# Zero passes on TensorE at the start, a third buffer in the early function, and 65 instead of 96 columns in the q' products

## The chip, the cores and the metric

The kernel runs on one core of one Trainium2 chip. The metric is the device time of one execution in microseconds (us), lower is better. TensorE is written PE in the profile, its weight loads PEld, VectorE DVE, ScalarE ACT, GpSimd POOL and SyncE SP. PE's clock has two levels here, 1.2 and 2.4 GHz.

## The reference

Three stages follow each other, all in float32. First comes a linear attention with random features (q, k, v of shape 2 x 8 x 576 x 64, 128 features):

```
h   = x_s @ omega.T - sum(x_s*x_s)/2          # x_s = q or k, scaled by 64**-0.25
phi = exp(h - max(h, -1)) / sqrt(128)         # gives q' and k'
kv  = k'.T @ v ;  z = sum over tokens of k'
out = (q' @ kv) / (q' @ z + 1e-6)
```

Its output, seen as 1152 tokens of 512 channels, is x of the second stage: `h = x @ w_in` (2048 wide), `g = h - tanh(h)`, `x = g @ w_out`. The third stage is a mixture of four dense experts: for each expert `relu(x @ w1[e]) @ w2[e]`, weighted by each token's normalised probability and summed.

## The kernel before

Products of weights and activations split every float32 operand in a high and a low part and add three products (high by high, high by low, low by high). The features are made by `features`: PE transposes blocks of 128 tokens (`psT`), ACT and DVE split them (`th`, `tl`, the helper `split`, lines 71 and 72), PE multiplies them by the transposed omega `ob` (`psP`), DVE takes the row maximum with its sign turned (`nm`, line 298), and ACT takes the exponential (`kf` or `qf`, line 302). `k_products` multiplies k' by v and by a block of ones (`psV`), so that z stands in the columns behind kv, and DVE copies the first `ZC` columns of each of four blocks to `kvz` (line 319). `q_products` transposes q' (`psQ`, copied by ACT to `qt`), and multiplies it by `kvz` (`psN`, line 348: 128 products of `ZC` = 96 columns, of which 65 are used; line 352: 32 products of half the weights with 65 columns). DVE adds 1e-6, takes the reciprocal and multiplies (lines 354 to 356), PE transposes back (`psX`), and ACT and DVE split the result to `x`, the second stage's input.

The first loads are issued by SP in program order: omega, two blocks of k (`kn`), the rest of k (`kr`, 128 tokens), v, and so on. PE's first work is the transpose of omega (`pso`), then four blocks of `kn`, then `kr` and the other blocks.

While the last q' units run, the second stage begins: `early` makes g = h - tanh(h) for three token ranges (512, 384 and 256 tokens) of the first four hidden blocks, twelve units in all. Its function `minus_tanh` has ten steps. For small h a polynomial is used and for others h - tanh(h): u (ACT: square of h), q (ACT, to y), t (ACT: tanh), m (ACT, a mask in u), a and b (DVE: the polynomial in y), s (DVE: h - tanh, line 453), c (DVE: copy s over y where u is not zero, line 454), h (ACT: high part) and l (POOL: low part, line 456). Before, s writes over h in the PSUM tile `pse`, and t, u and y have two buffers each.

Weights of the second stage arrive in a coded form of 64 bits: ACT and DVE decode them (`Decoded`: `y`, and `m` on lines 122, 126 and 127), ACT makes the high part and POOL the low part (`wal`, `wbl`, line 72).

Up to about 126 us the order of instructions on each engine is set by a scheduler that plans with its own costs. So a change of a size or of a buffer also moves instructions that the diff does not name. From there on PE, DVE and ACT follow an order written out in the program.

Of the kernel before, what the change touches and what calls it, by code (L numbers as in the profile page):

```python
# [8 lines left out]
F32 = mybir.dt.float32  # L9
F32R = mybir.dt.float32r  # L10
I32 = mybir.dt.int32
U32 = mybir.dt.uint32
AF = mybir.ActivationFunctionType
ALU = mybir.AluOpType
# [12 lines left out]
def tile_favor_attention__then__two_moe(  # L27
# [18 lines left out]
    nc = tc.nc  # L46
    B, H, S, D = q.shape
# [3 lines left out]
    E, _, F = w1.shape  # L51
    P = 128
# [21 lines left out]
    def run(todo):  # L74
        for step in todo:
            step()
# [107 lines left out]
    a2 = actx.enter_context(tc.tile_pool(name="a2", bufs=2))  # L184
    a3 = actx.enter_context(tc.tile_pool(name="a3", bufs=3))
    ps_t = actx.enter_context(tc.tile_pool(name="ps_t", bufs=2, space=bass.MemoryType.PSUM))
    ps_n = actx.enter_context(tc.tile_pool(name="ps_n", bufs=2, space=bass.MemoryType.PSUM))
    ps_p = actx.enter_context(tc.tile_pool(name="ps_p", bufs=2, space=bass.MemoryType.PSUM))
    kctx = ExitStack()
    kp = kctx.enter_context(tc.tile_pool(name="kp", bufs=2, side="right"))  # L190
    TD = TB * D
    VC = D + 1
    ZC = D + D // 2
    FULL = slice(0, TB * P)
    REST = slice(TB * P, S)

    def load_full(x, b, p, to):

        nc.sync.dma_start(out=to, in_=x[b, 2 * p:2 * p + 2, FULL, :].rearrange("h (r t) d -> r h (t d)", t=TB))
# [8 lines left out]
    def load_k(p):  # L208
        t = kp.tile([P, B, 2, TD], F32, tag="kn", name="kn")
        for b in range(B):  # L210
            load_full(k, b, p, t[:, b])
        return t
# [19 lines left out]
    def load_v(p):  # L232
        t = vs[p % 2]
        for b in range(B):
            load_full(v, b, p, t[:, b * 2 * TD:(b + 1) * 2 * TD].rearrange("p (h x) -> p h x", h=2))
            r = t[b * D:(b + 1) * D, VR + b * 2 * D:VR + (b + 1) * 2 * D].rearrange("p (h d) -> p h d", h=2)
            nc.sync.dma_start(out=r, in_=v[b, 2 * p:2 * p + 2, REST, :].rearrange("h r d -> r h d"))
# [8 lines left out]
    load_v(0)  # L246
    kn.append(load_k(1))
    load_v(1)

    pso = ps_t.tile([P, 512], F32, tag="t", name="pso")  # L250
    nc.tensor.transpose(pso[:, :P], om.rearrange("p j d -> p (j d)"), ident)
    oms = kp.tile([P, P], F32, name="oms", bufs=1)
    nc.scalar.mul(oms, pso[:, :P], scale)
# [3 lines left out]
    for j in range(2):  # L257
        r, c = slice(j * D, (j + 1) * D), slice(j * P, (j + 1) * P)
        split(ob[0][r, c], ob[1][r, c], oms[r, :])
    qn = ac.tile([P, B, H, TD], F32, name="qn")  # L260
    kvz = [ac.tile([P, B, 2, ZC], F32, name=f"kvz{p}") for p in range(NP)]

# [45 lines left out]
    def k_products(p, kf):  # L308
# [3 lines left out]
        def product(b, h):  # L312
# [5 lines left out]
            if (b, h) == (B - 1, 1):  # L318
                nc.vector.tensor_copy(kvz[p], ps[:, :, :, :ZC])
                if p + 2 < NP:  # L320
# [4 lines left out]
    def q_products(p, gs, qf):  # L325
# [15 lines left out]
        def attended(g):  # L341
            t0, c = gs[g]
            ps = ps_n.tile([P, 2, 2, P], F32, tag="n", name="psN")
            for j in range(c):
                t = t0 + j
                for h in range(2):
                    if t != TB:
                        nc.tensor.matmul(ps[:, j, h, :ZC], qt[g][:, j, h, :], kvz[p][:, t // (TB + 1), h, :], start=True, stop=True)  # L348
                        continue
# [68 lines left out]
    gs, po_of = {}, {}  # L418
# [5 lines left out]
    def new_g(i, j):  # L424
        pool = late["hpb"] if i % 2 or i >= NA else hpa
        gs[i, j] = tuple(pool.tile([P, N], F32R, tag="h" + z, name="h" + z) for z in "hl")

    def hidden(i, j, chunks=range(NC), bank=None, kks=range(KD)):
        if bank is None and chunks[0] == 0 and kks[0] == 0:
            ph[i, j] = late["ps_hb" if j % 2 else "ps_ha"].tile([P, NC, 512], F32, tag="h", name="psh")  # L430
        wh, wl = wa[i, j]
        for kk in kks:
            c = slice(kk * P, (kk + 1) * P)
            xh, xl = state["x"][kk]
            for z, (w, x) in enumerate(((wh, xh), (wh, xl), (wl, xh))):
                for n in chunks:
                    nc.tensor.matmul(  # L437
                        ph[i, j][:, n, :CH] if bank is None else bank, w[:, c],
                        x[:, n * CH:(n + 1) * CH] if bank is None else x[:, n],
                        start=z == 0 and kk == 0, stop=z == 2 and kk == KD - 1,  # L440
                    )

    def minus_tanh(ps, hh, hl, t, u, y, view, eng_lo):

        vec, act = nc.vector, nc.scalar
        return dict(
            u=lambda: act.activation(view(u), ps, AF.Square),
            q=lambda: act.activation(y, u, AF.Square, bias=ca),  # L448
            t=lambda: act.activation(view(t), ps, AF.Tanh),
            m=lambda: act.activation(u, u, AF.Relu, bias=ct),  # L450
            a=lambda: vec.scalar_tensor_tensor(out=y, in0=y, scalar=CB, in1=u, op0=ALU.add, op1=ALU.mult),  # L451
            b=lambda: vec.scalar_tensor_tensor(out=view(y), in0=view(y), scalar=C2, in1=ps, op0=ALU.mult, op1=ALU.mult),  # L452
            s=lambda: vec.tensor_tensor(out=ps, in0=ps, in1=view(t), op=ALU.subtract),  # L453
            c=lambda: vec.copy_predicated(view(y), view(u).bitcast(I32), ps),  # L454
            h=lambda: act.activation(hh, y, AF.Copy),  # L455
            l=lambda: (eng_lo or vec).tensor_tensor(out=hl, in0=y, in1=hh.bitcast(F32), op=ALU.subtract),  # L456
        )

    def activated(i, j, eng_lo=None):
        new_g(i, j)  # L460
        hh, hl = gs[i, j]
        ps = ph[i, j][:, :, :CH]
        if i < NA:
            t, u, y = (late["gp"].tile([P, N], F32, tag=z, name=z, bufs=1 + (z == "y")) for z in "tuy")
            g = minus_tanh(ps, hh, hl, t, u, y, grid, eng_lo)

            for n in range(NC):
                s = slice(n * CH, (n + 1) * CH)
                part = minus_tanh(ps[:, n], hh[:, s], hl[:, s], t, u[:, s], y[:, s], lambda z: z, eng_lo)
                g.update({x + str(n): part[x] for x in "chl"})  # L470
            return g
        return [
            lambda: nc.scalar.activation(grid(hh), ps, AF.Relu),
            lambda: nc.vector.scalar_tensor_tensor(  # L474
                out=grid(hl), in0=ps, scalar=0.0, in1=grid(hh).bitcast(F32), op0=ALU.max, op1=ALU.subtract
            ),
        ]

    def early(e):

        j, n = e % NJ, e // NJ
        if n == 0:
            new_g(0, j)
        s = slice(chunks[n][0][0] * P, (chunks[n][-1][0] + chunks[n][-1][1]) * P)
        w = s.stop - s.start
        pool, tag = (ps_p, "p") if e in (NP + 1, NP + 3, 2 * NP + 1) else (ps_e, "e")
        ps = pool.tile([P, 512], F32, tag=tag, name="pse")[:, :w]
        hidden(0, j, [s], ps)
        t, u, y = (a2.tile([P, 512], F32, tag=z, name=z)[:, :w] for z in "tuy")
        g = minus_tanh(ps, gs[0, j][0][:, s], gs[0, j][1][:, s], t, u, y, lambda z: z, nc.gpsimd)  # L490
        run(g[x] for x in "utqambsch" + "l")

    NU = len(q_units)
    for u in range(1, NU + 3):
        q_emit(u, "R", 0)
        q_emit(u - 1, "A", 0)
        q_emit(u - 2, "Z", 0)
        q_emit(u + 1, "T", 0)
        q_emit(u, "R", 1)
        q_emit(u - 1, "A", 1)  # L500
        q_emit(u - 2, "Z", 1)
        q_emit(u - 3, "X", 0)
        if u >= NP + 3:
            early(u - NP - 3)
        if u in LATER:
            ready(*LATER[u])
        if u == NU + 1:
            ready(load_a, wa, 1, 0)
    for e in range(NU - NP, NU):
        early(e)  # L510
        if e < NU - 2:
            ready(load_a, wa, 1, e % NJ + 1)
# [3 lines left out]
    for b in range(B):  # L516
        for t0, t1, r0, r1, s in token_rows(b):
            nc.sync.dma_start(
                out=pr[r0:r1, t0:t1, :],
# [192 lines left out]
    with tc.manual_schedule(engines={mybir.EngineType.DVE, mybir.EngineType.PE, mybir.EngineType.Activation}):  # L712
        coming = loads(0)
        opened(coming)
        g, left = None, []
        for n, (sh, so) in enumerate(order):
# [29 lines left out]
            g = activated(*steps[sh])  # L746
# [18 lines left out]
    for n in range(NC):  # L765
        s = slice(n * CH, (n + 1) * CH)
# [163 lines left out]
```

## Time and profile before

| | us |
|---|---|
| median of 3 runs | 681.74 |
| lowest and highest | 681.52, 682.08 |
| profiled execution | 681.03 |
| its span | 678.9 |

Of the span PE is busy for 666.2 us (98%), PEld 621.5, DVE 529.8, ACT 317.5, POOL 62.3. PE is called busy from the first to the last of a row of matmuls that follow each other closely, so a busy PE can still run at half its clock; the distance between the starts of two matmuls tells that. The page's line of the granted clock is at 9 tenths or more in all 40 slices; on the first 10 us the text below comes back to it. A row of the timeline gives start, duration, engine, line, what is written and read, and the count where several are merged; the bracket behind it tells how long the engine stood before it, and what released it.

### The profile page before, as it was taken

What the parts mean: (1) busy time and instruction counts of PE and PEld (TensorE: products, weight loads), DVE (VectorE), ACT (ScalarE), POOL (GpSimd) and SP (SyncE); (2) the same over time, 40 slices, a digit from 0 to 9 for tenths busy, and PEclk for the clock granted to TensorE, in tenths of its full rate; (3) what the DMA queues carried; (4) which work ended last, traced back from release to release, by engine and by line L of the source; (5) the groups of instructions that cost most, each with busy time, mean ns of one, the idle gap of its engine ahead of it and who ended that gap; (6) DMA issues with size and microseconds to landing.
All of it is one profiled execution on the core that took longest, in us unless ns stands there. A gap on an engine that the chain in (4) does not pass through costs nothing.

```text
span 678.9 us, 10154 instructions
## 1 busy us (share of the span) xinstructions
PE 666.2 (98%) x4059; PEld 621.5 (92%) x4059; DVE 529.8 (78%) x828; ACT 317.5 (47%) x593; POOL 62.3 (9%) x58
## 2 busy tenths in 40 slices
PE   6999999999999999999999999999999999999997
PEld 5999989999999999998999999998998999999986
DVE  4599889799999988968377777777777777777664
ACT  5699988857767756444122322222232223222120
POOL 1032023413212200100000000000000000000000
PEclk9999999999999999999999999999999999999999
DMA  8953201122322222121001111210202111110004
GB/s 225 281 169 119 67 32 32 32 62 95 94 63 93 78 79 63 31 63 32 1 31 63 32 49 45 63 33 32 63 31 63 32 63 32 36 58 1 1 0 140
DMA packets 42767, 43.73 MB, mean 64 GB/s; under 512 B 5600, under 2 KB 37600, under 8 KB 42720
## 3 DMA queue, kind: packets, MB, share of 16 engines
q1 hardware_dynamic: 42720, 43.08, 20.7%
q8 instruction: 32, 0.52, 0.3%
q14 instruction: 15, 0.12, 0.1%
HBM read 40.72 MB, written 2.36 MB: 63 GB/s over the span
## 4 chain that ended last, share of the span: by engine, by line
PE 79%; DVE 11%; ACT 5%; issue 2%; DMA 2%; SPq 1%; DVEq 0%
PE po L671 29%; PE Y L654 23%; PE po L550 7%; PE psh L437 7%; PE pse L437 4%; PE psP L296 3%; PE psN L348 2%; DVE m L127 1%; DVE m L126 1%; DVE y L451 1%; DVE y L452 1%; DVE y L454 1%; DVE psh L453 1%; ACT y L448 1%; PE psQ L337 1%
## 5 line engine op out<-in xcount | busy, mean ns | idle before, releaser
L677 DVE SCALAR_TENSOR_TENSOR oacc<-po,pr,oacc 128x512 f32<-128x512 f32 (+1 forms) x136 | 101.4, 746 | 34.3 <-PE po L671 33.8
L671 PE MATMUL po<-wbh,hl 128*128 128x512 f32 x290 | 113.0, 389 | 0.4 <-DVE hl L474 0.4
L671 PE MATMUL po<-wbh,hh 128*128 128x512 f32 x290 | 112.9, 389 | 0.1
L671 PE MATMUL po<-wbl,hh 128*128 128x512 f32 x290 | 112.9, 389 | 0.0
L671 PEld LDWEIGHTS po<-wbh,hl 128*128 128x128 f32 x290 | 54.4, 188 | 12.3 <-DVE hl L474 0.8
L671 PEld LDWEIGHTS po<-wbh,hh 128*128 128x128 f32 x290 | 54.7, 188 | 8.2 <-DVE oacc L677 0.3
L842 ACT ACTIVATE hh<-Y 128x576 fp32r<-128x576 f32 x42 | 27.4, 652 | 72.5 <-DVE Y L839 64.0
L671 PEld LDWEIGHTS po<-wbl,hh 128*128 128x128 f32 x290 | 54.4, 188 | 7.5
L550 PE MATMUL po<-hh,wbh 128*128 128x384 f32 x180 | 60.8, 338 | 0.3
L550 PE MATMUL po<-hl,wbh 128*128 128x384 f32 x180 | 60.7, 337 | 0.3 <-DVE hl L456 0.2
L550 PE MATMUL po<-hh,wbl 128*128 128x384 f32 x180 | 60.4, 336 | 0.0
L654 PE MATMUL Y<-y,wah 128*128 128x288 f32 x336 | 57.9, 294 | 0.0
L437 PE MATMUL psh<-x,wah 128*128 128x384 f32 x288 | 57.7, 336 | 0.0
L654 PEld LDWEIGHTS Y<-y,wah 128*128 128x128 f32 x336 | 51.2, 188 | 3.6 <-DVE hl L474 0.3
L437 PEld LDWEIGHTS psh<-x,wah 128*128 128x128 f32 x288 | 50.5, 188 | 0.0
L654 PE MATMUL Y<-Th,wal 128*128 128x288 f32 x224 | 47.9, 295 | 0.0
L654 PE MATMUL Y<-Tl,wah 128*128 128x288 f32 x224 | 47.6, 294 | 0.0
L654 PE MATMUL Y<-Th,wah 128*128 128x288 f32 x224 | 47.6, 293 | 0.0
L842 ACT ACTIVATE hh<-u 128x576 fp32r<-128x576 f32 x14 | 9.6, 687 | 73.5 <-DVE u L839 73.5
L654 PEld LDWEIGHTS Y<-Th,wah 128*128 128x128 f32 x224 | 39.0, 188 | 4.5
L455 ACT ACTIVATE hh<-y 128x1152 fp32r<-128x1152 f32 (+3 forms) x26 | 20.6, 796 | 41.4 <-DVE y L454 41.4
L624 ACT ACTIVATE wah<-y 128x512 fp32r<-128x512 f32 x28 | 17.6, 631 | 41.1 <-DVE y L604 41.1
(138 smaller groups left out, 1472.7 us busy)
## 6 DMA issues: line engine op xcount, KB each, us to landing
raw<-in_moe_w_dram SPq DMA_DIRECT2D x30, 512.0 KB, 3.5
raw<-in_moe_w_in_dram SPq DMA_DIRECT2D x16, 512.0 KB, 3.6
raw<-in_moe_w_out_dram SPq DMA_DIRECT2D x16, 512.0 KB, 3.4
kn<-in_k_dram SPq DMA_DIRECT2D x8, 256.0 KB, 3.9
vs<-in_v_dram SPq DMA_DIRECT2D x8, 256.0 KB, 4.3
qn<-in_q_dram SPq DMA_DIRECT2D x8, 256.0 KB, 4.9
out_dram<-oacc SPq DMA_DIRECT2D x7, 256.0 KB, 2.2
raw<-in_moe_w_dram SPq DMA_DIRECT2D x4, 256.0 KB, 3.2
```

The lines of the kernel that those rows point to most:

```text
L126: nc.vector.scalar_tensor_tensor(out=m, in0=self.y.bitcast(I32), scalar=3, in1=m, op0=ALU.logical_shift_left, op1=ALU.bitwise_or)
L127: nc.vector.scalar_tensor_tensor(out=m, in0=self.up, scalar=SIGN, in1=m, op0=ALU.bitwise_and, op1=ALU.bitwise_or)
L296: nc.tensor.matmul(ps[:, i].rearrange("p a m -> p (a m)"), x[:, c], o, start=j == 0, stop=j == 2)
L348: nc.tensor.matmul(ps[:, j, h, :ZC], qt[g][:, j, h, :], kvz[p][:, t // (TB + 1), h, :], start=True, stop=True)
L437: nc.tensor.matmul(ph[i, j][:, n, :CH] if bank is None else bank, w[:, c], x[:, n * CH:(n + 1) * CH] if bank is None else x[:, n], start=z ...
L455: h=lambda: act.activation(hh, y, AF.Copy),
L550: nc.tensor.matmul(po[:, :CH], w[:, r], g[:, s], start=j == 0 and z == 0, stop=j == NJ - 1 and z == 2,)
L624: nc.scalar.activation(w[0], src, AF.Copy)
L654: nc.tensor.matmul(ps[:, m, :HN // 2], w[:, kk], b[:, m * HN // 2:(m + 1) * HN // 2], start=first and kk == 0 and z == 0, stop=kk == 1 and ...
L671: nc.tensor.matmul(po, g[:, s], w[:, cols], start=j == 0 and z == 0, stop=j == 1 and z == 2)
L677: nc.vector.scalar_tensor_tensor(out=acc, in0=po, scalar=pr[:, t, e:e + 1], in1=acc, op0=ALU.mult, op1=ALU.add)
L842: nc.scalar.activation(halves(gs[NA + q, f][0][:, h * HN:(h + 1) * HN]), x, AF.Relu)
```

## The change

Three edits. (1) A tile of 128 x 256 zeros is filled by DVE, and PE multiplies it by itself 14 times ahead of everything else, into a PSUM tile of the pool `ps_n` that nothing reads. (2) In `early`, s writes its difference over the tanh in tile t instead of over h in PSUM, c reads it there, and y has three buffers instead of two. (3) `ZC` is 65 instead of 96, so line 348's products stream 65 columns, and the copy to `kvz` moves 260 elements a partition instead of 384.

```diff
-    ZC = D + D // 2
+    ZC = VC
...
+    zero = kp.tile([P, 2 * P], F32R, name="zero", bufs=1)
+    nc.vector.memset(zero.bitcast(F32), 0.0)
+    idle = ps_n.tile([P, 512], F32, tag="n", name="idle")
+
+    def busy(n):
+
+        for _ in range(n):
+            nc.tensor.matmul(idle[:, :2 * P], zero[:, :P], zero, start=True, stop=True)
+
 
     pso = ps_t.tile([P, 512], F32, tag="t", name="pso")
+    with tc.high_priority():
+        busy(14)
     nc.tensor.transpose(pso[:, :P], om.rearrange("p j d -> p (j d)"), ident)
...
-    def minus_tanh(ps, hh, hl, t, u, y, view, eng_lo):
+    def minus_tanh(ps, hh, hl, t, u, y, view, eng_lo, free=False):
+
 
         vec, act = nc.vector, nc.scalar
+        d = view(t) if free else ps
...
-            s=lambda: vec.tensor_tensor(out=ps, in0=ps, in1=view(t), op=ALU.subtract),
-            c=lambda: vec.copy_predicated(view(y), view(u).bitcast(I32), ps),
+            s=lambda: vec.tensor_tensor(out=d, in0=ps, in1=view(t), op=ALU.subtract),
+            c=lambda: vec.copy_predicated(view(y), view(u).bitcast(I32), d),
...
-        t, u, y = (a2.tile([P, 512], F32, tag=z, name=z)[:, :w] for z in "tuy")
-        g = minus_tanh(ps, gs[0, j][0][:, s], gs[0, j][1][:, s], t, u, y, lambda z: z, nc.gpsimd)
+        t, u, y = (a2.tile([P, 512], F32, tag=z, name=z, bufs=2 + (z == "y"))[:, :w] for z in "tuy")
+        g = minus_tanh(ps, gs[0, j][0][:, s], gs[0, j][1][:, s], t, u, y, lambda z: z, nc.gpsimd, free=True)
```

PE at the program's start, before and then after (line numbers behind the edit are higher by 11 to 13):

```order
L251 MATMUL pso<-ident,om 128x128
L284 MATMUL psT<-ident,kn 128x128 x4
L284 MATMUL psT<-ident,kr 128x128
L284 MATMUL psT<-ident,kn 128x128 x3
L296 MATMUL psP<-ob_130,th 128x256 x2
```

```order
L256 MATMUL idle<-zero 128x256 x14
L262 MATMUL pso<-ident,om 128x128
L295 MATMUL psT<-ident,kn 128x128 x4
L295 MATMUL psT<-ident,kr 128x128
L295 MATMUL psT<-ident,kn 128x128 x3
L307 MATMUL psP<-ob_147,th 128x256 x2
```

The 14 passes stand ahead of the transpose of omega; the order behind them is the same.

DVE between the third and the fourth copy to `kvz`, before and then after (nm: row maxima; tl: low part of a transposed block; m: decoding of weights):

```order
L319 COPY kvz_141<-psV 128x384
L298 TENSOR_REDUCE nm<-psP 128x4
L127 SCALAR_TENSOR_TENSOR m<-raw,m 128x512
L298 TENSOR_REDUCE nm<-psP 128x4
L72 TENSOR_TENSOR tl<-psT,th 128x512
L126 SCALAR_TENSOR_TENSOR m<-y,m 128x512
L122 TENSOR_SCALAR m<-raw 128x512
L298 TENSOR_REDUCE nm<-psP 128x4
L127 SCALAR_TENSOR_TENSOR m<-raw,m 128x512
L126 SCALAR_TENSOR_TENSOR m<-y,m 128x512
L72 TENSOR_TENSOR tl<-psT,th 128x512
```

```order
L330 COPY kvz_158<-psV 128x260
L309 TENSOR_REDUCE nm<-psP 128x4
L127 SCALAR_TENSOR_TENSOR m<-raw,m 128x512
L309 TENSOR_REDUCE nm<-psP 128x4
L126 SCALAR_TENSOR_TENSOR m<-y,m 128x512
L72 TENSOR_TENSOR tl<-psT,th 128x512
L127 SCALAR_TENSOR_TENSOR m<-raw,m 128x512
L122 TENSOR_SCALAR m<-raw 128x512
L309 TENSOR_REDUCE nm<-psP 128x4
L126 SCALAR_TENSOR_TENSOR m<-y,m 128x512
L122 TENSOR_SCALAR m<-raw 128x512
L72 TENSOR_TENSOR tl<-psT,th 128x512
```

One more decoding step of line 122 stands ahead of the fourth copy, and a tl comes one step later.

DVE in an early unit of 512 tokens, before and then after (steps a, b, s and c are lines 451 to 454, then 464 to 467):

```order
L451 SCALAR_TENSOR_TENSOR y<-y,u 128x512
L355 RECIPROCAL rd<-rd 128x2
L355 RECIPROCAL rd<-rd 128x4
L452 SCALAR_TENSOR_TENSOR y<-y,pse 128x512
L453 TENSOR_TENSOR pse<-pse,t 128x512
L356 TENSOR_TENSOR xs<-psN,rd 128x128
L454 COPY_PREDICATED y<-u,pse 128x512
```

```order
L464 SCALAR_TENSOR_TENSOR y<-y,u 128x512
L365 TENSOR_SCALAR rd<-psN 128x2
L465 SCALAR_TENSOR_TENSOR y<-y,pse 128x512
L466 TENSOR_TENSOR t<-pse,t 128x512
L366 RECIPROCAL rd<-rd 128x2
L365 TENSOR_SCALAR rd<-psN 128x4
L467 COPY_PREDICATED y<-u,t 128x512
```

Step c now reads u and t, both in SBUF; before, one of its two inputs was in PSUM.

## Rows read from the trace of the kernel before

**Rows 1.** Busy time by stretch: length, then each engine's busy us and count

```profile
core 0: us, PE busy (x) PEld busy (x) DVE busy (x) ACT busy (x) POOL busy (x), PEclk, DMA share, GB/s
14.00:31.00 17.00, 16.56 (x140) 16.01 (x138) 9.47 (x17) 11.64 (x41) 0.00 (x0) 1.00 0.91 271
31.00:51.00 20.00, 18.80 (x157) 18.01 (x157) 19.96 (x35) 18.92 (x55) 6.53 (x5) 1.00 0.62 188
51.00:126.00 75.00, 74.98 (x562) 70.19 (x563) 65.73 (x169) 68.11 (x178) 19.72 (x18) 1.00 0.18 57
126.00:679.00 553.00, 547.96 (x3160) 510.12 (x3158) 430.11 (x598) 212.48 (x307) 33.79 (x23) 1.00 0.16 51
```

**Rows 2.** Timeline of the first 9 us, DVE and PE

```profile
0.87 0.55 DVE L256 MEMSET ob<- 128x256 f32 x2 [0.87 <-PEq L914]
...
2.79 0.45 PE L251 MATMUL pso<-ident,om 128*128 128x128 f32 x1 [2.79 <-DMA om<-in_omega_dram]
...
4.52 1.11 PE L284 MATMUL psT<-ident,kn 128*128 128x128 f32 x4 [1.28 <-DMA kn<-in_k_dram]
...
7.62 0.45 PE L284 MATMUL psT<-ident,kr 128*128 128x128 f32 x1 [1.99 <-DMA kr<-in_k_dram]
7.86 0.85 PE L284 MATMUL psT<-ident,kn 128*128 128x128 f32 x3
```

**Rows 3.** Timeline from 8.7 us: how the first features are made

```profile
8.75 0.92 ACT L71 ACTIVATE th<-psT 128x512 fp32r<-128x512 f32 x2 [1.95 <-PE psT L284]
...
9.38 0.89 DVE L72 TENSOR_TENSOR tl<-psT,th 128x512 fp32r<-128x512 f32 x2 [1.87 <-ACT th L71]
...
10.45 1.52 DVE L298 TENSOR_REDUCE nm<-psP 128x4 f32<-128x512 f32 x2 [0.19 <-PE psP L296]
...
10.97 0.28 PE L296 MATMUL psP<-ob,tl 128*128 128x256 f32 x1
...
11.18 2.17 ACT L302 ACTIVATE kf<-psP,nm 128x128 f32<-128x128 f32 x8 [1.51 <-DVE nm L298]
```

**Rows 4.** The same view as rows 1, behind the last matmul

```profile
676.00:681.00 5.00, 0.00 (x0) 0.00 (x0) 0.00 (x0) 0.00 (x0) 0.00 (x0) 0.88 0.11 35
```

**Rows 5.** Timeline from 20 us: SP's issues, and who waits for one

```profile
20.55 0.37 SPq L199 DMA_DIRECT2D vs<-in_v_dram  x1
...
24.66 0.47 SPq L103 DMA_DIRECT2D raw<-in_moe_w_in_dram  x1
...
30.70 0.43 DVE L122 TENSOR_SCALAR m<-raw 128x512 int32<-128x512 int32 x1 [2.31 <-DMA raw<-in_moe_w_in_dram]
```

**Rows 6.** DVE's groups by shape, 0 to 137 us: busy us, mean ns

```profile
L298 DVE TENSOR_REDUCE nm<-psP 128x2 f32<-128x256 f32 x8 | 3.4, 422 | 2.1 <-PE psP L296 2.1
...
L319 DVE COPY kvz<-psV 128x384 f32<-128x384 f32 x4 | 2.2, 548 | 0.2 <-PE psV L314 0.2
```

**Rows 7.** Timeline of PE, one q' unit

```profile
60.34 0.60 PE L337 MATMUL psQ<-ident,qf 128*128 128x128 f32 x4
60.77 1.03 PE L348 MATMUL psN<-kvz,qt 128*128 128x96 f32 x8
```

**Rows 8.** Waits from 68 to 126 us: us in total, times, longest

```profile
ACT y L448 <- POOL hl L456: 1.1, 2, 0.9
```

**Rows 9.** Timeline: DVE steps beside a POOL subtraction, and one without

```profile
74.64 1.27 POOL L72 TENSOR_TENSOR wal<-m,wah 128x512 fp32r<-128x512 f32 x1 [6.67 <-ACT wah L71]
...
75.20 1.26 DVE L126 SCALAR_TENSOR_TENSOR m<-y,m 128x512 int32<-128x512 int32 x1
...
81.16 0.68 DVE L126 SCALAR_TENSOR_TENSOR m<-y,m 128x512 int32<-128x512 int32 x1
...
116.96 1.29 POOL L72 TENSOR_TENSOR wal<-m,wah 128x512 fp32r<-128x512 f32 x1 [0.29 <-ACT wah L71]
117.37 0.60 DVE L454 COPY_PREDICATED y<-u,pse 128x384 f32<-128x384 int32 x1 [0.52 <-ACT u L450]
```

**Rows 10.** The instructions of line 122: ns min/median/max, first and last start

```profile
L122 DVE TENSOR_SCALAR m<-raw x11: 398/428/1516, 30.7 to 80.7; 128x512 int32<-128x512 int32 x11
```

## The prediction

> **What bounds the kernel now.** I read the busy times by stretch first, then the timeline of the start, then the groups by shape and the waits of the stretches that the change touches. The busy times by stretch [rows 1] show that PE has next to no gap once it runs: it stands still for 17.00 - 16.56 = 0.44 us between 14 and 31 us, for 1.20 us between 31 and 51, and for 0.02 us in the 75 us after that. From 126 us on the change touches nothing, and PE is busy for 547.96 of 553 us there. So whatever edits 2 and 3 save on DVE or ACT can shorten the program by no more than 0.44 + 1.20 + 0.02 = 1.66 us, unless PE itself gets through its work faster. In 31 to 51 us DVE is busy for 19.96 of 20 us and ACT for 18.92, so there DVE sets the pace beside PE.
>
> The start is another matter. PE waits for loads until 7.62 us [rows 2], and then it works at half its speed: three transposes take 0.85 us, of which the last one alone is about 0.43, so their starts lie 0.21 us apart. In the q' part four transposes of the same size take 0.60 us with 0.27 for the last, 0.11 apart [rows 7]. A factor of two between these is that of 1.2 to 2.4 GHz, though the granted clock that the profile prints has no dip at the start: the paces tell it.
>
> **The change part by part.**
>
> *Zero passes.* DVE's first memset starts at 0.87 us and two take 0.55 [rows 2], so the zeros are there at about 1.15 and PE begins at about 1.3. I price a pass like a transpose at that clock, 0.21 us: 14 x 0.21 = 2.9 us, so they end near 4.2. The transpose of omega, at 2.79 before, comes behind them, at about 4.25, and its 0.45 us end at 4.7. Behind it the queue holds the four blocks of kn, which wait for their load until 4.52 anyway [rows 2]: 0 us lost. The scaling of omega on ACT follows at 4.75 and is done before the first transposes are (4.52 + 0.6). The memsets of ob move by 0.27 us on an otherwise idle DVE. All this is hidden by the loads; without that cover it would be 2.9 us.
>
> What it brings begins at 7.62. If the clock is up by then, the four transposes start 0.11 apart: 7.62 + 3 x 0.11 + 0.27 = 8.22 instead of 7.86 + 0.85 = 8.71, 0.48 us earlier with ACT's start, at 8.75 before [rows 3]. ACT's split and DVE's tl keep their durations, so tl ends 0.48 earlier, and the 0.19 us that the maxima then waited for PE [rows 3] goes as well, since the products are ahead by more. The maxima start 0.48 + 0.19 = 0.67 us earlier, and so do the eight exponentials at 11.18, which from there on ACT runs without a gap, with PE waiting for k' behind them. Does it last to 126 us? Between 14 and 31 us PE is busy at 16.56 of 17 us, so it carries the lead on. The one place where it could get lost is the load of the first weights: DVE waited 2.31 us for it until 30.70 [rows 5]. It is issued at 24.66, at the end of a row of issues without a pause that begins at 20.55, when PE has read the first v. PE's lead moves that row too. I take 0.65 us. The lower end is 0 (no higher clock at 7.62, or the lead lost at that load). The upper end: all that PE does from 7.62 to 10.97, where a product is down to 0.28 us [rows 3], at double speed: 3.35/2 = 1.7 us.
>
> Will the clock still be up after the wait from about 5.1, where the four fast transposes would end, to 7.62? At the end of the program the mean clock over 676 to 681 us is 0.88 with no matmul in it [rows 4]: with half clock as the lower level it stayed up for at least 3.8 us of idleness. A gap of 2.5 us is less. Before the change PE had worked from 7.62 to shortly before 10.97, some 3 us, when the pace rose, and the 14 passes are about as much work. I hold both likely, together at 0.8.
>
> *Copies to kvz.* 548 ns for 384 elements and 422 for 256 of another operation out of PSUM [rows 6] make 0.98 ns an element; 124 fewer save 0.12 us a copy. Two of the four lie in 31 to 51 us, where DVE sets the pace: 0.24 us at most, and since PE has little room there I take 0.15 (0 to 0.5).
>
> *65 columns.* Eight products of 96 columns take 1.03 us: (1.03 - 0.28)/7 = 0.107 us apart. Transposes of 128 columns with the same 128 x 128 weights are (0.60 - 0.27)/3 = 0.11 apart [rows 7]. A third more columns cost nothing, so the columns are not what is waited for, and 65 save nothing: 0 us. If the pace did go with the columns, it would be 128 x 0.107 x 31/96 = 4.4 us; the equal paces speak against it. The Trainium skill, TensorE: Matmul & The Clock Gate, section Back-to-back issue gap, has an isolated matmul's gap go with its columns, N/2.4 + 2.5 ns; by that the sum would gain an estimated 128 x 31/2.4 ns = 1.65 us. The measured 0.107 us for 96 columns does not agree with it: it would be 0.043.
>
> *Early function.* The third buffer takes away ACT's waits of 1.1 us in total for POOL [rows 8]; PE stood still for 0.02 us in that whole stretch [rows 1], so they cost PE nearly nothing: 0.1 us (0 to 0.3). The difference in SBUF frees the PSUM tile one step earlier, and PE does not wait there either: 0. Against it stands step c, which now reads two tiles in SBUF. Line 126, which has two such inputs, takes 0.68 us alone and 1.26 when it starts inside a POOL subtraction (it ends 0.55 us behind it); step c with one input in PSUM started inside one at 117.37 and took its usual 0.60 [rows 9]. So each of the 12 c's that meets POOL will be longer by up to 0.6, at worst by the 1.28 of the subtraction. DVE has 75 - 65.73 = 9.3 us to spare in that stretch [rows 1], which covers five or six such meetings (3.5 us): 0 us, with bounds of 0 and 12 x 1.28 - 9.3 = 6 us.
>
> The Trainium skill says the same as a rule, SBUF — State Buffer, section Who interferes with whom: a DVE instruction with two SBUF inputs contends with a GpSimd instruction that reads SBUF, and one of them blocks fully. By that rule c would be delayed in each meeting and the sum be worse by what DVE cannot hide; rows 9 agree for line 126, and no row here shows it for this operation.
>
> *The scheduler's new order.* DVE has one more step of line 122 ahead of the fourth copy: 0.43 us alone, 1.52 at worst [rows 10]; in exchange one less follows. I take 0, between -0.6 and +1.1 us.
>
> Sum on the profiled execution's time: 681.03 - 0.65 - 0.15 - 0.1 = 680.13. The median of the runs is 0.71 above that execution, so the time is 681.74 - 0.9 = **680.8 us**.
>
> **The rivals.**
> 1. The clock is not up at 7.62, or the lead ends at the load of the weights: 681.74 - 0.25 = 681.5. For it: 2.5 us of pause, and loads with a DMA share of 0.91 in 14 to 31 us. Against: rows 4, and SP's issues that follow PE.
> 2. The new order also closes the gaps that are left: 681.74 - 0.65 - 1.66 = 679.4. For it: DVE and ACT are nearly full between 31 and 51, and the change frees both a little. Against: 1.2 of the 1.66 us hang on a load and on DVE's decoding, which stay.
> 3. The products of 65 columns do run faster: 680.8 - 1.6 to - 4.4, so about 678. The equal paces speak against it.
> 4. Step c, now with two SBUF inputs, is blocked by POOL, in the stretch of 85 to 126 us. It decides the time as soon as DVE falls behind the early units by more than its spare time: if the meetings come close together, six of 0.6 us, 3.6 us in all, reach PE: 680.8 + 3.6 = 684.4, slower. For it: rows 9. Against: 9.3 us of spare time. The extra step of line 122, at its worst 1.1 us, works in the same direction.
>
> **How the numbers follow.** A measurement of this kernel can tell about 0.2%, 1.36 us, from no change. The forecast has 0.52, rival 1 has 0.18, rival 2 0.19, rival 3 0.04, rival 4 0.07. Faster than 680.38: rivals 2 and 3 and 0.05 of the forecast's own spread, 0.28. Slower than 683.1: rival 4, 0.07. The rest, 0.65, is within 0.2%. The range leaves out a part of rivals 2 to 4: 679.3 to 682.2; the forecast's own is 680.2 to 681.4.
>
> **What would show it.** In the changed profile the passes stand from 1.3 to about 4.2 us, the transposes behind the load of kr lie 0.11 apart, and the first exponentials start at about 10.5 instead of 11.18; the DVE step that waited for the weights starts at about 30.05 instead of 30.70; line 348's products stay at 0.107 apart; the copies take 0.42; some c's take 1.0 or more beside POOL; PE's busy time in 51 to 126 us stays full. The forecast is wrong if the transposes at 7.62 are still 0.21 apart, if the wait at 30.70 keeps its place, or if PE shows gaps of more than a us behind 51 us.

## The result and the profile after

The changed kernel takes 685.27 us (684.30 to 686.91, six runs), the kernel before 681.57 beside it: a ratio of 1.0056, 95% interval 1.0043 to 1.0069. It is 3.7 us slower; 680.8 was predicted. Its profiled execution has a span of 682.7 us.

The busy times by stretch, with the columns of [rows 1]:

```profile
core 0: us, PE busy (x) PEld busy (x) DVE busy (x) ACT busy (x) POOL busy (x), PEclk, DMA share, GB/s
14.00:31.00 17.00, 15.75 (x133) 15.21 (x131) 8.92 (x18) 11.26 (x40) 0.00 (x0) 1.00 0.94 283
31.00:51.00 20.00, 19.00 (x156) 17.97 (x156) 19.57 (x34) 17.99 (x53) 6.19 (x5) 1.00 0.56 174
51.00:126.00 75.00, 71.91 (x540) 66.51 (x540) 67.43 (x162) 65.52 (x170) 17.15 (x15) 1.00 0.18 56
126.00:679.00 553.00, 551.86 (x3182) 513.97 (x3181) 433.68 (x604) 216.20 (x317) 35.60 (x26) 1.00 0.16 50
```

From 51 to 126 us PE now stands still for 75 - 71.91 = 3.09 us, where it stood still for 0.02. Behind 126 us it has 551.86 - 547.96 = 3.90 us more to do than at the same moment before, and that is the loss. Between 14 and 31 us PE stands still for 1.25 us, where it stood still for 0.44. From 51 to 126 us DVE works longer (67.43 against 65.73 us) and gets through fewer instructions (162 against 169).

The start (start, duration, engine, line, what; the bracket is the idle time before, and what ended it):

```profile
1.20 3.35 PE L256 MATMUL idle<-zero 128*128 128x256 f32 x14 [1.20 <-DVE zero L250]
...
4.80 1.12 PE L295 MATMUL psT<-ident,kn 128*128 128x128 f32 x4
...
7.50 0.49 PE L295 MATMUL psT<-ident,kn 128*128 128x128 f32 x3
...
9.46 1.28 DVE L309 TENSOR_REDUCE nm<-psP 128x4 f32<-128x512 f32 x2
...
10.17 2.17 ACT L313 ACTIVATE kf<-psP,nm 128x128 f32<-128x128 f32 x8 [1.38 <-DVE nm L309]
...
30.26 0.43 DVE L122 TENSOR_SCALAR m<-raw 128x512 int32<-128x512 int32 x1 [2.69 <-DMA raw<-in_moe_w_in_dram]
```

The three transposes of kn take 0.49 us instead of 0.85 [rows 2], the first maxima start at 9.46 instead of 10.45 [rows 3], the exponentials at 10.17 instead of 11.18, and DVE gets the first weights at 30.26 instead of 30.70 [rows 5]. So far the forecast has the direction right, but a single profile tells little about the first weights: e11 below, a kernel with the start and the order of before, has them at 32.36, 1.7 us later than the kernel before itself. Step by step against before, DVE is still 0.55 us ahead at 45.5 us (the same row maximum starts at 45.50 instead of 46.05) and 2.3 us behind at 61 (60.71 instead of 58.41). Between lies this (DVE, POOL and PE):

```profile
44.84 0.42 DVE L122 TENSOR_SCALAR m<-raw 128x512 int32<-128x512 int32 x1
...
45.13 2.98 POOL L72 TENSOR_TENSOR wal<-m,wah 128x512 fp32r<-128x512 f32 x2 [6.23 <-ACT wah L71]
...
46.88 1.51 DVE L122 TENSOR_SCALAR m<-raw 128x512 int32<-128x512 int32 x1
...
50.11 0.41 DVE L330 COPY kvz<-psV 128x260 f32<-128x260 f32 x1
...
50.33 1.27 POOL L72 TENSOR_TENSOR wbl<-m,wbh 128x512 fp32r<-128x512 f32 x1 [2.22 <-ACT wbh L71]
50.45 1.70 DVE L126 SCALAR_TENSOR_TENSOR m<-y,m 128x512 int32<-128x512 int32 x1
...
51.41 0.51 PE L307 MATMUL psP<-ob,th 128*128 128x256 f32 x2 [0.75 <-ACT qf L313]
...
54.09 0.41 PE L348 MATMUL psQ<-ident,qf 128*128 128x128 f32 x2 [0.64 <-DVE tl L72]
...
55.89 1.00 PE L359 MATMUL psN<-kvz,qt 128*128 128x65 f32 x8
```

Line 122 at 46.88 takes 1.51 us and line 126 at 50.45 takes 1.70, where they take 0.43 [rows 10] and 0.68 [rows 9] alone: they start inside a POOL subtraction and end 0.3 to 0.6 us behind it (45.13 + 2.98 = 48.11, 50.33 + 1.27 = 51.60). PE then waits for an exponential whose row maximum (49.51) stands behind line 122 on DVE, and for a tl (53.27) that stands behind both. Before, one line 122 met POOL in this place too and took as long,

```profile
44.61 1.52 DVE L122 TENSOR_SCALAR m<-raw 128x512 int32<-128x512 int32 x1
```

but line 126 started later in the subtraction beside it (at 51.09, 1.16 us). A second place follows in the early function:

```profile
103.32 1.30 POOL L469 TENSOR_TENSOR hl<-y,hh 128x512 fp32r<-128x512 f32 x1 [4.55 <-ACT hh L468]
...
103.89 1.28 DVE L464 SCALAR_TENSOR_TENSOR y<-y,u 128x512 f32<-128x512 f32 x1 [0.66 <-ACT y L461]
...
108.78 1.60 POOL L469 TENSOR_TENSOR hl<-y,hh 128x512 fp32r<-128x512 f32 x1 [4.15 <-ACT hh L468]
...
109.23 1.56 DVE L464 SCALAR_TENSOR_TENSOR y<-y,u 128x384 f32<-128x384 f32 x1
```

These are two steps a (`y<-y,u`, two inputs in SBUF), each held until POOL is done; alone the sizes take 0.68 and 0.55 us. The waits of PE from 51 to 126 us (what waited for what: us, times, longest) show who pays:

```profile
PE pse L448 <- DVE t L466: 1.4, 2, 0.8
PE psP L307 <- ACT qf L313: 1.0, 2, 0.8
```

The first row is new in kind: the products of an early unit wait until DVE's step s has read the PSUM tile that they want.

### The profile page after: what moved, and what is told of

Its sections match the earlier page's. It is cut to its first block, busy times and chain, and to the rows that moved or that the text cites. A ratio compares the mean times of both kernels' runs of the same rounds, so it can differ in the third digit from the quotient of the medians.

```text
span 682.7 us, 10182 instructions
## 1 busy us (share of the span) xinstructions
PE 669.0 (98%) x4073; PEld 623.0 (91%) x4073; DVE 535.7 (78%) x829; ACT 318.1 (47%) x593; POOL 61.2 (9%) x58
## 4 chain that ended last, share of the span: by engine, by line
PE 75%; DVE 14%; ACT 5%; issue 2%; DMA 2%; SPq 1%; DVEq 0%
PE po L684 29%; PE Y L667 23%; PE po L563 7%; PE psh L448 7%; PE psP L307 2%; PE pse L448 2%; DVE y L464 2%; DVE y L467 2%; DVE y L465 2%; DVE m L126 1%; PE psN L359 1%; DVE m L127 1%; ACT y L461 1%; DVE psh L466 1%; ACT m L117 1%
```

## The experiments

Most experiments part the edits from the order of the instructions. A kernel is held to an order like this: a table of ranks, taken from the built program whose order is wanted, chains the instructions of PE, ACT, DVE and POOL up to the written order, engine by engine, with edges that carry no semaphore. It does not hold the steps of one weight of the written part that fall in that stretch, on DVE a line 126 and a line 127: in e2 (e9, e12 and e15 are like it) this line 126 starts at 91.60 us (before 105.51), in e3 the two start at 97.47 and 108.29 (changed kernel 108.54 and 116.91), in e10 line 127 starts at 109.11. In e11, e13 and e14 all of DVE's steps stand as in the kernel whose order is wanted.

```
ORDER = dict(PE=[0, 1, 2, ...], Activation=[...], DVE=[...], Pool=[...])
...
        for a, b in zip(ranks, ranks[1:]):
            tc.add_manual_dep(ins[b], ins[a].name, mybir.DependencyInfo(mybir.DependencyClass.NoSync, ...), reason="order")
```

"Ratio" is to the kernel before, timed beside it on the same chip, with its 95% interval.

| run | content | order | median us | ratio |
|---|---|---|---|---|
| e1 | edit 1 alone | before | 680.99 | 0.9998 (0.9989 to 1.0006) |
| e2 | all edits | before | 681.10 | 0.9998 (0.9989 to 1.0007) |
| e3 | no edit | changed kernel | 686.97 | 1.0083 (1.0069 to 1.0096) |
| e4 | 65 columns alone | its own | 689.25 | 1.0114 (1.0099 to 1.0129) |
| e5 | all edits | changed to 65 us, then before | 683.48 | 1.0035 (1.0023 to 1.0047) |
| e6 | all edits | before to 65 us, then changed | 683.33 | 1.0029 (1.0018 to 1.0039) |
| e7 | all, no low parts on POOL | changed kernel | 680.03 | 0.9989 (0.9976 to 1.0001) |
| e8 | all, no low parts on POOL | before | 679.68 | 0.9975 (0.9962 to 0.9987) |
| e9 | all, 14 more passes | before | 679.28 | 0.9975 (0.9967 to 0.9984) |
| e10 | all, s and c as before | changed kernel | 685.39 | 1.0068 (1.0051 to 1.0084) |
| e11 | 65 columns alone | before | 680.94 | 0.9998 (0.9988 to 1.0009) |
| e12 | e9, two moves in its order | before, but for these | 679.81 | 0.9980 (0.9970 to 0.9990) |
| e13 | all, 5 POOL steps later | changed kernel | 683.92 | 1.0043 (1.0030 to 1.0056) |
| e14 | all, 9 POOL steps later | changed kernel | 682.06 | 1.0017 (1.0008 to 1.0026) |
| e15 | e9, 3 POOL steps later | before | 679.01 | 0.9965 (0.9953 to 0.9977) |

**The edits or the order.** Edit 1 alone needs no table: the scheduler keeps the order of before. e2 and e3 cross the two.

> Edit 1 alone (the 14 passes over zeros); the order of every other instruction is that of before. Order theory (the loss comes from the new order of the instructions up to 126 us, and the passes bring what the changed profile showed, 0.44 us at the first weights): 681.57 - 0.44 = 681.1 us, between 680.6 and 681.3. Step-c theory (the loss comes from POOL blocking the DVE step that now has two SBUF inputs): the same 681.1. Rival (the passes themselves cost the time, by the clock or by the memory that they read): 684 to 685.5.

> All three edits, but PE, DVE, ACT and POOL are held to the order of before up to the order written out in the program. Order theory: 681.57 - 0.44 for the start - 0.1 to 0.3 for the shorter copies = 680.9 us (680.4 to 681.5). Step-c theory: the loss stays, 684.5 to 685.5. Width or memory layout (65 columns, the third buffer and where it lies): the loss stays, 684.5 to 685.5.

> None of the three edits, but PE, DVE, ACT and POOL are held to the order of the changed kernel. Order theory: the whole loss and the start's gain is missing, 681.57 + 3.7 + 0.44 = 685.7 us (684.5 to 687, more where the two y buffers make ACT wait in this order). Step-c theory: c reads PSUM here, so the loss is gone: 681.6 to 682.5.

> Edit 3 alone (65 columns), in the order that the scheduler then chooses, which differs from both. Order theory: no fixed number, it is another draw; if it shares the changed kernel's first part (one more decoding step ahead of the fourth copy) some 683 to 686 us, in any case not 681.57 - 0.2. Step-c theory: 681.4 (c reads PSUM). Width theory: if the products of 65 columns are faster, 680 or less.

All three edits in the order of before cost nothing; no edit at all in the changed kernel's order costs 0.83%, 5.7 us. So the loss is that of the order, and neither the passes nor step c nor the width makes it. The fourth run shows that the width is enough to set the scheduler off: `ZC = VC` alone gives DVE the changed kernel's order up to about 100 us, and the order that it gets behind that, without edit 2, is worse still. Edit 2 was not run alone. e11, the same code in the order of before, closes this:

> 65 columns alone, held to the order of before. The width itself: 0 us from the products (their pace is that of the weight loads), 0.1 to 0.3 from the four shorter copies: 681.0 us (680.7 to 681.3). With its own order the same kernel took 689.25. If the width itself or the memory layout did the harm: above 684.

0.9998 against 1.0114: the same instructions, 1.16% or 7.9 us apart by their order. And the 65 columns themselves bring nothing that can be measured.

**Where the order loses.** The two orders hold the same instructions up to 65 us on PE, ACT and DVE, so they can be cut there and joined.

> All three edits. PE, DVE and ACT are held to the changed kernel's order up to about 65 us and to the order of before from there on. The traces show the changed kernel losing in two places: DVE goes from 0.55 us ahead of before at 45.5 us to 2.3 us behind at 61, and from 2.3 behind at 98 to 4.0 behind at 126. If these are two losses of their own: 681.1 (the second run's kernel) + 2.0 = 683.1 us, between 682.3 and 684. If the first loss makes the second: about 685. If the first is made good by slack that PE and DVE have until 126 us: 681 to 681.8.

> The other half: the order of before up to about 65 us, the changed kernel's from there on. Two losses of their own: 681.1 + 1.8 = 682.9 us (682.2 to 683.6). If the second loss comes only from being late: 681 to 681.6. If the second is the whole loss: 685.

Two losses of their own: against e2 (0.9998) 0.37% and 0.31%, 2.5 and 2.1 us, where the changed kernel has 0.58% in all. PE's busy time from 51 to 126 us points the same way, if less in e6, whose profiled execution was the fastest of its eleven: idle for 0.43 us in e2,

```profile
51.00:126.00 75.00, 74.57 (x564) 69.76 (x563) 68.38 (x169) 68.75 (x181) 20.77 (x18) 1.00 0.19 60
```

for 2.20 us in e5,

```profile
51.00:126.00 75.00, 72.80 (x549) 67.78 (x550) 67.07 (x165) 67.20 (x174) 18.71 (x17) 1.00 0.19 56
```

and for 1.15 us in e6:

```profile
51.00:126.00 75.00, 73.85 (x554) 68.73 (x553) 67.34 (x166) 66.88 (x174) 20.35 (x17) 1.00 0.18 55
```

**What makes the loss there.** First POOL's low parts are left out up to the written order (`late` is empty till then):

```diff
         def parted(self):
             hi, lo = halves_of(wp, self.tag)
+            if not late:
+                nc.scalar.activation(hi, self.m.bitcast(F32), AF.Copy)
+                return hi, hi
...
-        run(g[x] for x in "utqambsch" + "l")
+        run(g[x] for x in "utqambsch")
+        gs[0, j] = gs[0, j][:1] * 2
```

> All three edits in the changed kernel's order, but up to the order written out in the program POOL makes no low parts: the low part of the weights and of g is left out there, and the high part is read in its place, so the same products run. No DVE step can then meet a POOL subtraction. Meeting theory (the new order is worse because its decoding and early steps run beside POOL's subtractions, up to 1.1 us longer each): the difference to the next run, the same with the order of before, falls from 4.2 us to under 1: about 680.5 to 681.5 us. Order theory without meetings (the steps simply stand in a worse order): 684.5 or more, still some 4 us above the next run.

> The same without POOL's low parts (left out up to the written order, the high part read in their place) in the order of before. Both theories: 680 to 681 us, since few meetings were on the path before; it is the other side of the comparison with the run before it.

The two orders, 0.58% apart with POOL at work (1.0056 and 0.9998), are 0.14% apart without it, with overlapping intervals. In the new order without POOL's work PE stands still for 0.29 us from 51 to 126 us, instead of 3.09:

```profile
51.00:126.00 75.00, 74.71 (x562) 69.76 (x561) 64.27 (x169) 68.36 (x179) 0.53 (x1) 1.00 0.18 55
```

The order of before gains as well, 0.23% or 1.6 us against e2: POOL's subtractions cost time there too, and both runs came out below what was expected. But with the subtractions go also the waits for them. So e13 and e14 keep every instruction and its order, and let only the POOL steps begin later:

```diff
+    LATER_POOL = {3: 82, 4: 95, 5: 107, 6: 120, 7: 198, 10: 168, 11: 183, 13: 195, 14: 206}
+    for k, r in LATER_POOL.items():
+        tc.add_manual_dep(pool[k], dve[r].name, mybir.DependencyInfo(mybir.DependencyClass.Sync, ...), reason="later")
```

(POOL's subtraction number k waits for DVE's instruction of rank r; e13 has the first five.)

> The changed kernel in its own order; five POOL subtractions (the fourth to the eighth) may begin only behind a DVE step, so that none of the decoding steps of 46 to 69 us starts beside one. Meeting theory: the five steps (0.85, 1.51, 1.70, 0.96, 1.15 us, and 1.30 at 67.9) go back to 0.43 and 0.68, 2.2 us of DVE time more than in the order of before are gone, and the first of the two losses (2.4 us) goes for the greater part: 685.3 - 1.4 to 2.4 = 683.4 us. If the order loses by itself, or by the other waits on POOL: 685.3 +- 0.4, or more, since POOL is later.

> As the run before, and four more POOL subtractions of 103 to 122 us behind step a (103.9 and 109.2, 1.28 and 1.56 us), the decoding step of 117 and a step c. Meeting theory: the second loss (2.0 us) goes for the greater part too: 682 us, between 681.2 and 682.8. If only the first place hangs on meetings: as the run before, 683.4. If neither does: 685 or more.

The changed kernel lies 0.56% above before, e13 0.43%, e14 0.17%: work that begins later gives back 0.9 and 2.7 of 3.8 us (e13's interval still overlaps the changed kernel's, e14's doesn't). e13's 0.9 us is less than the 1.4 to 2.4 expected, so its time alone doesn't show the first place's share. Its profile does show the wait gone there: from 51 to 85 us PE stands still for 0.36 us (changed kernel 1.34), from 85 to 126 us, where nothing was moved, for 1.75 as in the changed kernel:

```profile
51.00:85.00 34.00, 33.64 (x281) 31.14 (x282) 28.68 (x77) 31.34 (x87) 6.40 (x5) 1.00 0.28 89
85.00:126.00 41.00, 39.25 (x267) 36.17 (x266) 37.83 (x86) 34.62 (x85) 12.60 (x11) 1.00 0.09 27
```

In e14's timeline most of the same DVE steps stand alone:

```profile
46.52 0.41 DVE L122 TENSOR_SCALAR m<-raw 128x512 int32<-128x512 int32 x1
...
48.27 1.29 POOL L72 TENSOR_TENSOR wal<-m,wah 128x512 fp32r<-128x512 f32 x1 [2.23 <-DVE m L127]
...
48.99 1.11 DVE L126 SCALAR_TENSOR_TENSOR m<-y,m 128x512 int32<-128x512 int32 x1
...
101.81 0.69 DVE L464 SCALAR_TENSOR_TENSOR y<-y,u 128x512 f32<-128x512 f32 x1 [0.68 <-ACT y L461]
...
102.58 1.31 POOL L469 TENSOR_TENSOR hl<-y,hh 128x512 fp32r<-128x512 f32 x1 [5.90 <-DVE y L464]
...
107.17 0.56 DVE L464 SCALAR_TENSOR_TENSOR y<-y,u 128x384 f32<-128x384 f32 x1 [0.17 <-ACT y L461]
...
108.20 1.30 POOL L469 TENSOR_TENSOR hl<-y,hh 128x512 fp32r<-128x512 f32 x1 [4.31 <-DVE xs L367]
```

Its busy times from 51 to 126 us:

```profile
51.00:126.00 75.00, 73.76 (x552) 68.39 (x551) 65.48 (x167) 67.61 (x175) 20.40 (x17) 1.00 0.16 51
```

Line 122 takes 0.41 instead of 1.51 us, the steps a 0.69 and 0.56 instead of 1.28 and 1.56, and PE stands still for 1.24 us instead of 3.09. Line 126 at 48.99 still meets a subtraction (1.11 us). What is left between e14 and e2, 0.19% or 1.3 us, may be the meetings that remain, the order itself or POOL's delay; these runs don't part the three.

The sum of what DVE is held up does not tell the time of a kernel. An estimate from the traces (each DVE step's time beyond what the same step takes clear of POOL, 31 to 126 us) gives 3.2 us before, 8.8 in the changed kernel, 5.7 in e2, 4.4 in e14, 6.8 in e3 and 6.3 in e4; yet e3 and e4 lose more than the changed kernel, and e2 nothing. So it is not the sum that counts; that it is the place of the meetings is not shown. What e3 and e4 lose beside them is open; both have two y buffers and s in PSUM, and PE's longest wait in e4 (31 to 126 us) is 1.3 us for a step c that reads PSUM.

**Step c.** e10 gives `early` back the s and c of before (`free=True` is left out):

> The changed kernel in its own order, but s writes its difference to PSUM again and c reads it there (the passes, 65 columns and the third buffer stay). What share step c with two SBUF inputs has in the loss: if c is one of the steps that POOL holds up, the c's longer by 0.1 to 0.7 us behind 120 us go back to their 0.45 to 0.76, and the time is 685.3 - 0.5 to 1.2 = 684.4 us; if the loss is that of the other steps alone (decoding, step a), 685.3 +- 0.3; if c were the whole second loss, 683.3.

1.0068, no better than the changed kernel: the 684.4 us expected for a share of c were missed. Its profile still has a 1.28 at 103.75, and at 109.11 line 127, which the table doesn't hold, takes the place of step a and is held up itself:

```profile
103.75 1.28 DVE L461 SCALAR_TENSOR_TENSOR y<-y,u 128x512 f32<-128x512 f32 x1 [0.69 <-ACT y L458]
...
108.64 1.59 POOL L466 TENSOR_TENSOR hl<-y,hh 128x512 fp32r<-128x512 f32 x1 [4.15 <-ACT hh L465]
...
109.11 1.67 DVE L127 SCALAR_TENSOR_TENSOR m<-raw,m 128x512 int32<-128x512 int32 x1
```

So e10 alone doesn't clear step c. e2 does for the order of before: four of its c's are held up there, by 1.9 us in all (1.34 us at 118.52, where 384 elements take 0.60 alone), and it takes no longer than the kernel before. The c's of the changed kernel get longer beside POOL too (1.47 us at 121.51 for 384 elements); no run shows a share of the loss in them.

**The start.** e1 had no gain, though its passes ran as planned. Its timeline (the first fence), and its busy times from 8 to 11 us (the second, with the granted clock ahead of the DMA share):

```profile
4.46 0.60 PE L294 MATMUL psT<-ident,kn 128*128 128x128 f32 x4
...
7.39 0.49 PE L294 MATMUL psT<-ident,kn 128*128 128x128 f32 x3
...
9.39 0.41 PE L306 MATMUL psP<-ob,th 128*128 128x256 f32 x1
...
10.36 1.95 ACT L312 ACTIVATE kf<-psP,nm 128x128 f32<-128x128 f32 x7 [1.52 <-DVE nm L308]
```

and

```profile
8.00:11.00 3.00, 3.00 (x16) 3.00 (x16) 1.89 (x4) 1.44 (x5) 0.00 (x0) 0.50 1.01 298
```

The clock is up for the transposes at 7.39, and from 8 to 11 us, behind 2.19 us in which PE waited for kr, the granted clock is 0.50: the products take 0.41 us instead of 0.28. Of the ten profiles with 14 passes, six show a granted clock of 0.50 to 0.68 from 8 to 11 us (e1, e5 to e8, e10), two more still have products of 0.41 us there without a record (e2, e14; their transposes lie 0.21 apart from the first on, so the clock had not risen), and two have the clock up there: the changed kernel's, where the first four transposes were still 0.21 apart, and e13's. e9 fills the wait:

```diff
+    FILL = 14
...
-        busy(14)
+        busy(14 + FILL)
```

(The 14 more stand behind the first four transposes of kn.)

> All three edits in the order of before, and 14 more passes over zeros behind the four transposes of kn, where PE waits for kr (2.2 to 2.4 us). In most runs with 14 passes the clock rose at 4 to 6 us and fell again behind that wait. If the pause is what lets it fall: the clock is up from about 4.4 us on without a fall, the first exponentials start at 10.1 to 10.5 instead of 11.2, and if the lead lasts, 681.1 - 0.5 = 680.6 us (680.2 to 681). If the lead ends at the load of the first weights (landing at 30.3 to 31.9 in the runs so far, whatever PE does): the clock as above but 681.1 +- 0.3. If the clock falls all the same: no change at all.

Its timeline, PE and ACT at the start and DVE at the first weights:

```profile
5.27 2.19 PE L257 MATMUL idle<-zero 128*128 128x256 f32 x14
...
7.51 0.49 PE L296 MATMUL psT<-ident,kn 128*128 128x128 f32 x3
...
10.18 2.18 ACT L314 ACTIVATE kf<-psP,nm 128x128 f32<-128x128 f32 x8 [1.38 <-DVE nm L310]
...
29.52 0.43 DVE L122 TENSOR_SCALAR m<-raw 128x512 int32<-128x512 int32 x1 [1.94 <-DMA raw<-in_moe_w_in_dram]
```

All three profiles with the filled wait (e9, e12, e15) keep the clock up. The exponentials start at 10.18, the first weights are there at 29.52, and the kernel takes 0.25% less than before, and 0.23% or 1.6 us less than e2, from which it differs by these passes alone; 0.5 us less than e2 was expected. The three have the first weights at 29.14 to 29.52, ahead of the other 14 profiles (29.56 to 32.36), so the lead lasts. That the load follows PE's clock is not shown: e10 has them at 29.56 with the clock down at 8 to 11 us, e13 at 30.72 with it up.

Two attempts to go on from there:

> The ninth run's kernel with two moves in the order: DVE takes the row maxima of 128x2 ahead of the first decoding step, and ACT three exponentials ahead of the step that reads the same weights, both of which stood behind the wait for the first weights (DVE 2.3 us, ACT 1.1, PE 1.08 in rows of before). If PE's 1.08 us there is on the path: 0.4 to 1 us less than the ninth run, about 680.2. If DVE, full from 31 to 51 us, sets the pace behind it: only the 0.42 us of the moved step, or nothing: 680.6.

```diff
 L72 TENSOR_TENSOR tl<-psT,th 128x128
-L122 TENSOR_SCALAR m<-raw 128x512
 L310 TENSOR_REDUCE nm<-psP 128x2
+L122 TENSOR_SCALAR m<-raw 128x512
 L126 SCALAR_TENSOR_TENSOR m<-y,m 128x512
```

> The ninth run's kernel (679.28: all edits, order of before, 14 more passes), with three POOL subtractions of 32 to 50 us let begin behind the decoding steps that they held up (1.26, 1.52 and 1.16 us; one of the three will still meet a step for 0.4). Meeting theory: up to 2 us of DVE time less in a stretch where DVE is full; without any POOL work the order of before gained 1.4 us, so 679.3 - 0.5 to 1.4 = 678.4 us. If PE has no gap there to give back: 679.3.

e12's moves brought nothing (0.9980 against 0.9975), which fits DVE, full behind that wait, setting the pace. e15 (`{0: 33, 2: 80, 4: 107}` for the table above) is the fastest at 679.01, but its interval overlaps e9's, so a gain over e9 isn't shown; one meeting went over from line 122 to the line 126 that follows it (1.48 us at 33.6).

## Why the prediction was wrong

**The step that failed** is "The scheduler's new order ... I take 0, between -0.6 and +1.1 us". It measured +4.0 us (changed kernel against e2, 0.58%) to +5.7 (e3 against before). The loss does begin beside the extra step of line 122 ahead of the fourth copy, but that step took its 0.42 us there (44.84), and the 1.51 of the next one stands for the 1.52 of before: line 122 takes 6.5 us in all, before 6.6. What was wrong was to price one moved step. The order had moved many, and their meetings with POOL were not counted: line 126 has a mean of 876 ns over its 13 instructions up to 137 us, before 762. The groups by shape after (busy us, mean ns), with the copies,

```profile
L126 DVE SCALAR_TENSOR_TENSOR m<-y,m 128x512 int32<-128x512 int32 x13 | 11.4, 876 | 0.2 <-DVE m L122 0.2
...
L122 DVE TENSOR_SCALAR m<-raw 128x512 int32<-128x512 int32 x11 | 6.5, 603 | 2.7 <-DMA raw<-in_moe_w_in_dram 2.7
...
L330 DVE COPY kvz<-psV 128x260 f32<-128x260 f32 x4 | 1.7, 418 | 0.2 <-PE psV L325 0.2
```

and before:

```profile
L126 DVE SCALAR_TENSOR_TENSOR m<-y,m 128x512 int32<-128x512 int32 x13 | 9.9, 762 | 0.0
...
L122 DVE TENSOR_SCALAR m<-raw 128x512 int32<-128x512 int32 x11 | 6.6, 610 | 2.3 <-DMA raw<-in_moe_w_in_dram 2.3
```

**The cover that wasn't there.** "DVE has 75 - 65.73 = 9.3 us to spare in that stretch" is a sum over 75 us, and the meetings come in two bunches, where DVE has none: from 44 to 54 us it goes from step to step with a pause of 0.24 us at most. For step c, which that sentence was about, the cover held in e2. PE's 0.02 us of idleness was read as a limit to what can be gained; read the other way it says that PE has no slack, and every us that it waits once stays lost.

**Rival 4** (0.07, 684.4 us) had the mechanism, POOL blocking a DVE step with two SBUF inputs. Its 3.6 us, nearly the size measured, is luck: it is a sum over six meetings of step c, and in e2 the c's meet POOL and cost nothing. It was the decoding and step a, which the edits don't touch. That they meet POOL was in [rows 9] and [rows 10], and only the order decides how often.

**Zero passes.** They ran from 1.20 to 4.55 us, (3.35 - 0.41)/13 = 0.23 apart against 0.21 priced. In the changed kernel's profile the lead is 1.01 us at the first exponentials (0.67 predicted) and 0.44 at the first weights (0.65 predicted): PE's 1.25 us of standing still from 14 to 31 us contradict that it "carries the lead on". In e1's times the gain is 0.1 us (-0.4 to 0.7): in its profile the clock falls behind the wait of 2.2 us. The transposes of kn began at 4.80, not at 4.52, which the wait for kr hid. [rows 4] didn't tell: there the clock had been up for hundreds of us before the pause. Kept up (e9) it is worth 1.6 us, near the upper end of 1.7.

**Copies, columns, buffer.** The copies take 418 ns (0.42 predicted); the 0.15 and 0.1 us priced for them and for the third buffer are too small for these runs to show. Eight products of 65 columns take 1.00 us, (1.00 - 0.28)/7 = 0.103 apart against 0.107 [rows 7], and e11 shows no gain: rival 3 is out, and the sum by the isolated gap of the Trainium skill (TensorE: Matmul & The Clock Gate, Back-to-back issue gap), an estimated 1.65 us, doesn't come either; that section itself says that the isolated gap comes out too short for a small product that loads its weights, and these do. On POOL the rule of the Trainium skill (SBUF — State Buffer, Who interferes with whom) holds, but not for step c alone: any DVE instruction with two SBUF inputs is at risk beside POOL, and the rows above show it for step a and lines 126 and 127. The same section counts DVE's tensor_scalar in its fast modes in; line 122, which has one tensor input, agrees: held up by 1.51 - 0.42 = 1.09 us. Whether it runs in such a mode no run here shows.

## What to carry to other kernels

Where a scheduler sets the order, a change of a size is a change of the order, and that can cost more than the edit can bring: hold the order fixed to time an edit, and time the orders apart. On an engine without slack look for where its suppliers bunch; a sum of spare time over a long stretch covers nothing. Steps that hold each other up can be moved apart in time with the order kept: beginning nine POOL subtractions later gave back 2.7 of 3.8 us.

## What the runs showed of the hardware

- The hold-up goes both ways: in the kernel before a POOL subtraction that starts at 48.50, just behind line 127 (48.45), takes 1.78 us, alone 1.27.
- Even a DVE step of 9 elements a partition (`sm`, line 537), 0.14 us alone in the kernel before, takes 1.02 us beside a POOL subtraction of 1.02; in e6, at 113.80, it takes 0.18, and the subtraction beside it and the line 127 that follows takes 1.69:

```profile
115.94 1.02 POOL L469 TENSOR_TENSOR hl<-y,hh 128x384 fp32r<-128x384 f32 x1 [1.38 <-ACT hh L468]
115.98 1.02 DVE L537 TENSOR_SCALAR sm<-sm 128x9 f32<-128x9 f32 x1
```

- The granted clock is printed as 1.00 up to the first change that the profile holds, even where the paces show half of it: in e2 the four transposes behind the kr wait at 7.99 start 0.21 apart under a printed 1.00.
- 14 passes (3.3 us of work, then a pause of 1.4 to 2.6 us) raise the clock ahead of the products in eight of ten profiles, and in six of these it is back at half for some or all of 8 to 11 us; with 28 passes, and no pause over 0.4 us up to the first products, it rose and stayed up in three of three.
